# Splitting the weights of a transformer block on GpSimd for each chunk, in place of storing split weights in DRAM

## The chip, the cores and the metric

The kernel runs on one core of a Trainium2 chip. The metric is the time of one execution on the device in microseconds (us), as the median of several runs.

## The reference, cut to what matters

One block on x of shape [1, 2048, 512], all in float32: a layer norm that is scaled and shifted by rows made from a condition c, attention with 32 heads of width 16, a second modulated norm, and a gated feed-forward part of width 1792 (SwiGLU).

```python
mod = (_silu(c) @ w_mod).reshape(c.shape[0], 6, 1, -1)
sa, ca, ga, sb, cb, gb = (mod[:, i] for i in range(6))
h = _layernorm(x) * (1 + ca) + sa
x = x + ga * attention(h, wqkv, wo)          # softmax over all 2048 keys, 32 heads
h = _layernorm(x) * (1 + cb) + sb
x = x + gb * ((silu(h @ w_gate) * (h @ w_up)) @ w_down)
```

## The kernel before, in words

**Split operands.** Dense products run on TensorE (PE) in the type float32r. To keep float32 accuracy each operand is kept as two tiles, a high part `hi` (the value rounded to float32r by a copy) and a low part `lo` (the value minus `hi`), and each product is three matmuls: hi·hi, hi·lo, lo·hi. Making the two parts is "splitting": one copy and one subtraction.

**Tiling.** The 2048 rows are four chunks of 512 (`NC`, `CW`). First comes the projection to q, k and v, which go to DRAM in split form. Attention then runs in 32 units (`NU`): 8 groups of 4 heads for each chunk. A unit has 16 steps; in a step PE makes four score tiles for the row maximum 21 steps ahead (L479, reduced by VectorE, DVE, at L481), four score tiles for the current keys (L506, exponentials on ScalarE, ACT, L508) and the products with v (L521). `kop` and `qop` hold the keys and queries of a unit; half of their loads are issued by GpSimd (POOL) and half by SyncE (SP) at L404.

**Chunk work between the attention steps.** When the eight units of a chunk have ended, its output projection with `wo`, its second norm and its feed-forward part are done during the units of the next chunk. `plain(steps)` emits attention steps alone; `filled(places, work)` emits eight pairs of attention matmuls with matmuls of `work` put between them. The feed-forward part of a chunk is a list of jobs: `gate_up(f)` for f = 0 to 13 (gate and up columns of 128, tile `wgu` with gate and up, hi and lo), and `down(m)` for m = 0 to 6, twice for each m (tile `wd` with two blocks of 128 rows, hi and lo). The order is gate_up 0, 1, 2, down 0, gate_up 3, 4, down 1, and so on to gate_up 13, down 6. A gate_up takes two `filled` calls and each half of a down one. In this stage the matmuls are cut in halves of 64 rows (L719). After the last attention step the last seven jobs of chunk 2 and all of chunk 3 run alone (`whole`, full matmuls at L729).

**Tiles and loads.** `wgu` has two buffers, `wd` one, `mid` (the split product of gate and up) three. `load_gu(f + 1)` is issued on SP when gate_up f begins, `load_wd(m + 1)` on SP when down m has ended. In the last chunk six places are used for `wgu`, four of them in `kop` tiles that are free by then, and loads run four ahead. A unit that closes (`close_unit`) sends its sum through DRAM to get it in the shape of a row: SP issues `dn`, `d_dr` and `rb` (L542), then POOL multiplies `on = o * rb` (L548) and stores it (L549).

**Where the split weights come from.** During the first eight units a generator `split_weights` loads the plain weights into `mid` tiles on the POOL queue (L579), multiplies `wo` by ga and `w_down` by gb / 2 (L605, L621), splits them on POOL (copy L583, subtraction L584), and stores hi and lo to DRAM (`wo_dr`, `gu_dr`, `wd_dr`, L587). `after(i)` advances it at three of 16 steps. Each chunk then loads hi and lo, 1 MB for each `wgu` and `wd`, at L646, L652 and L657.

**Other splits.** The product of gate and up is split at L781 and L782: on POOL during attention, on ACT and DVE in `whole`. The attention output of a chunk is split on POOL at L667 and L668, the turned normed rows at L706 and L707.

**Order.** Every engine runs its instructions in the order in which the program emits them, under manual scheduling, and waits by semaphore. A POOL or ACT instruction that waits holds all that are emitted after it.

Of the kernel before, what the change touches and what calls it, by code (L numbers as in the profile page):

```python
# [9 lines left out]
F32 = mybir.dt.float32  # L10
# [9 lines left out]
P = 128  # L20
S = 2048
D = 512
# [4 lines left out]
NK = D // P  # L27
NC = 4
CW = S // NC
NG = H // 4  # L30
NU = NG * NC
NF = F // P
FG = 2
# [9 lines left out]
UG = 16 * NG  # L43
# [11 lines left out]
def run(it):  # L55
    for _ in it:
        pass


def take(it, k):  # L60
    run(islice(it, k))
# [40 lines left out]
def block_kernel(ctx, tc, x, wqkv, wo, w_gate, w_up, w_down, c, w_mod, out):  # L102
    nc = tc.nc
# [447 lines left out]
    def at(i, f):  # L551
        due.setdefault(i, []).append(f)
# [19 lines left out]
    def as_wo(w):  # L572
        return w.rearrange("p (b k) x c -> p b k (x c)", b=2)

    def split_weights():

        def raw(src, k):
            t = tile_mid().bitcast(F32)
            nc.gpsimd.dma_start(t.rearrange("p e c -> p (e c)").rearrange("p (k c) -> p k c", k=k), src)  # L579
            return t  # L580

        def parts(hi, lo, t):
            nc.gpsimd.tensor_copy(hi, t)  # L583
            nc.gpsimd.tensor_sub(lo, t, hi.bitcast(F32))  # L584

        def store(dst, w):
            nc.gpsimd.dma_start(dst, w.bitcast(F32))  # L587

        def cols(m):
            return slice(m * FG * P, (m + 1) * FG * P)  # L590

        srcs = [(wod[:, 2 * k:2 * k + 2, :], 2) for k in range(NK // 2)]
        for m in range(NF // FG):
            srcs += [(wgd[:, :, cols(m)], NK), (wud[:, :, cols(m)], NK), (wdd[:, m * FG:(m + 1) * FG, :], FG)]
        ahead = [raw(*srcs.pop(0)) for _ in range(2)]
        yield

        def following():
            if srcs:
                ahead.append(raw(*srcs.pop(0)))  # L600
            return ahead.pop(0)

        for k in range(NK // 2):
            t = following()
            nc.gpsimd.tensor_mul(t, t, ga_bc[:, None, :].to_broadcast([P, 2, D]))  # L605
            w = tile_gu()
            parts(as_wo(w)[:, 0], as_wo(w)[:, 1], t)
            store(wo_dr[k], as_wo(w))
            yield
        for m in range(NF // FG):  # L610
            ws = [tile_gu() for _ in range(FG)]
            for e in range(2):
                t = following()
                src = t.rearrange("p e c -> p (e c)").rearrange("p (k f c) -> p f k c", k=NK, f=FG)
                for f in range(FG):
                    parts(ws[f][:, 2 * e], ws[f][:, 2 * e + 1], src[:, f])
                    if e:
                        store(gu_dr[m * FG + f], ws[f])
                yield
            t = following()  # L620
            nc.gpsimd.tensor_mul(t, t, gb_bc[:, None, :].to_broadcast([P, FG, D]))  # L621
            w = tile_wd()
            parts(w[:, 0], w[:, 1], t)
            store(wd_dr[m], w)
            yield

    class Chunk:
        def __init__(self, ci, x2, oT, hT):
            self.ci, self.x2, self.oT, self.hT = ci, x2, oT, hT
            self.w, self.wd, self.mid, self.mv, self.nt = {}, {}, {}, None, []  # L630
            self.places, self.ahead, self.loaded = None, 1, set()
            self.jobs = [(gate_up, (0,)), (gate_up, (1,))]
# [10 lines left out]
        def load_wo(self, places=None):  # L643
            self.wo = places or [as_wo(tile_gu()) for _ in range(NK // 2)]
            for k, w in enumerate(self.wo):
                (nc.gpsimd if self.ci == last else nc.sync).dma_start(w.bitcast(F32), wo_dr[k])  # L646

        def load_gu(self, f):
            if f < NF and f not in self.loaded:
                self.loaded.add(f)  # L650
                self.w[f] = self.places[f % len(self.places)] if self.places else tile_gu()
                nc.sync.dma_start(self.w[f].bitcast(F32), gu_dr[f])  # L652

        def load_wd(self, m):
            if m < NF // FG:
                self.wd[m] = tile_wd()
                nc.sync.dma_start(self.wd[m].bitcast(F32), wd_dr[m])  # L657

        def load_o(self, eng, ks=range(NK)):
            for k in ks:  # L660
# [164 lines left out]
    def scaled(ch):  # L825
        ch.load_gu(0)
        ch.norm_scale(nc.gpsimd)
        ch.nt = [tile_mid().bitcast(F32) for _ in range(2)]
        for t in range(4):
            ch.normalize(t)  # L830

    def hook():
        while posts:
            posts.pop(0)()
# [32 lines left out]
    weights2 = split_weights()  # L867

    def after(i):
        nonlocal pf  # L870
        for f in due.pop(i, []):
            f()
        j = i + LEAD
        if j % 16 == 15 and j < n:
            max_rows(j // 16)
        if i == -2:
            run(late)
            sm.finish()
            es_a0.close()
# [90 lines left out]

    at(n - 24, begin_last)
    at(n - 13, lambda: chunks[last].load_o(nc.gpsimd, range(NK - 1)))
    at(n - 11, lambda: chunks[last].split_o(range(NK - 1)))
    outs = [banks[b] for b in FBANKS]
    for ci in range(last):
        plain(STARTS[ci] - done // 4)
        ch = chunks[ci]
        for t0 in (0, 2):
            work = out_pair(ch, t0, outs, True)
            filled(TWO, work)  # L980
            filled(TWO, work)
        side.append(lambda: scaled(ch))
        plain(NORM)
        plain(WIN, [lambda tp, k=k: ch.turned(tp, k) for k in range(NK)])
        if ci == last - 1:
# [8 lines left out]
    chunks[last - 1].load_gu(NF - 2)  # L994
    filled((0,) * 4, iter(()))


    assert done == 4 * n
# [68 lines left out]
```

## Time and profile before

| | us |
|---|---|
| median of 3 runs | 1879.55 (1879.51 to 1881.34) |
| span of the profiled execution, first to last instruction | 1875.6 |
| PE busy | 1846.7 (98%) |
| DVE busy | 1541.8 (82%) |
| ACT busy | 1252.4 (67%) |
| POOL busy | 415.3 (22%) |

The time outside the span, taken as the median minus the span, is about 4.0 us. How to read the rows that follow: a group of instructions has a line, an engine, an operation, the tiles that it writes and reads, the shape, the count, busy us, mean ns of one, and the idle time of the engine in front of it with what ended it. A timeline row has the start, the time that it covers, and in brackets the idle time in front. A matmul's end is modelled, so starts of matmuls are the better clock: in the last stage they are 0.23 us apart.

### The profile page before, as it was taken

How to read it: one execution, taken by the hardware profiler on the slowest of the kernel's cores; microseconds unless marked ns; L12 is line 12 of the kernel's file. 1: busy time of each engine (PE TensorE's matmuls, PEld its weight loads, DVE VectorE, ACT ScalarE, POOL GpSimd, SP SyncE). 2: the span in 40 equal slices, each digit the busy share in tenths (PEclk: the TensorE clock that was granted, in tenths of full speed). 3: DMA queues.
4: the chain of work that ended last, by engine and by line, in shares of the span. 5: the costliest groups of instructions: out<-in, count | busy, mean ns of one | idle time of the engine just before them, and what ended most of it. 6: DMA issues, size and time to landing. Idle time of an engine off the chain costs nothing.

```text
span 1875.6 us, 41002 instructions
## 1 busy us (share of the span) xinstructions
PE 1846.7 (98%) x16996; PEld 1160.4 (62%) x16996; DVE 1541.8 (82%) x2558; ACT 1252.4 (67%) x2406; POOL 415.3 (22%) x498
## 2 busy tenths in 40 slices
PE   7999999999999999999999999999999999999999
PEld 5766444444455766666555667666554566667887
DVE  5548999999999888888999888889999988831643
ACT  4221888888887766777777776677878877674211
POOL 3000454456323211111133111111123011030200
PEclk9999999999999999999999999999999999999999
DMA  8855677766843534554454454453643446243642
GB/s 286 292 198 142 174 183 178 201 167 190 211 86 78 145 102 124 144 124 90 107 124 116 108 127 131 121 122 78 159 86 56 108 92 156 86 159 119 249 180 110
DMA packets 78854, 267.62 MB, mean 143 GB/s; under 512 B 17364, under 2 KB 22484, under 8 KB 57988
## 3 DMA queue, kind: packets, MB, share of 16 engines
q1 hardware_dynamic: 59820, 180.10, 33.0%
q0 software_dynamic: 18160, 84.10, 19.0%
q8 instruction: 133, 2.18, 0.5%
q10 hardware_dynamic: 688, 0.80, 0.1%
q14 instruction: 53, 0.43, 0.1%
HBM read 201.85 MB, written 62.13 MB: 141 GB/s over the span
## 4 chain that ended last, share of the span: by engine, by line
PE 95%; DVE 2%; ACT 2%; DMA 0%; issue 0%; SPq 0%; ACTq 0%; DVEq 0%
PE bank L521 26%; PE bank L506 22%; PE bank L719 19%; PE bank L479 10%; PE bank L729 7%; PE bank L209 7%; DVE mx L481 1%; PE bank L762 1%; PE bank L491 1%; PE bank L162 0%; PE bank L703 0%; DMA wm_ab<-in_w_mod 0%; DVE stt L745 0%; PE bank L279 0%; PE bank L493 0%; PE bank L492 0%
## 5 line engine op out<-in xcount | busy, mean ns | idle before, releaser
L481 DVE TENSOR_REDUCE mx<-bank 128x1 f32<-128x512 f32 x2048 | 1286.5, 682 | 119.5 <-PE bank L479 72.4
L479 PE MATMUL bank<-kop,qop 48*128 48x512 f32 x2048 | 748.0, 432 | 3.6 <-DVE mx L481 3.4
L506 PE MATMUL bank<-qop,kop 50*128 50x512 f32 x2048 | 742.1, 427 | 4.6 <-ACT pt__20499 L508 0.5
L506 PEld LDWEIGHTS bank<-qop,kop 50*128 50x128 f32 x2048 | 347.0, 184 | 305.6 <-issue 63.3
L479 PEld LDWEIGHTS bank<-kop,qop 48*128 48x128 f32 x2048 | 343.9, 184 | 30.7 <-DVE mx L481 14.4
L719 PE MATMUL bank<-act,wgu 64*128 64x512 f32 x1872 | 297.9, 392 | 0.0
L719 PEld LDWEIGHTS bank<-act,wgu 64*128 64x128 f32 x1872 | 188.4, 187 | 30.9 <-DVE m L779 0.3
L548 POOL TENSOR_TENSOR on<-o,rb 128x512 f32<-128x512 f32 x31 | 39.7, 1282 | 442.9 <-DMA rb<-d_dr 304.0
L719 PE MATMUL bank<-wd,mid 64*128 64x512 f32 x912 | 136.5, 397 | 0.0
L781 POOL CAST mid<-m 128x512 fp32r<-128x512 f32 x40 | 24.3, 609 | 430.1 <-PE bank L479 165.5
L719 PEld LDWEIGHTS bank<-wd,mid 64*128 64x128 f32 x912 | 93.3, 185 | 12.0 <-issue 0.8
L209 PE MATMUL bank<-hT,wqs 128*128 128x512 f32 x384 | 95.7, 399 | 2.1 <-DVE prt L369 0.8
L209 PEld LDWEIGHTS bank<-hT,wqs 128*128 128x128 f32 x384 | 70.3, 188 | 24.3 <-issue 6.1
L777 DVE SCALAR_TENSOR_TENSOR q<-th,bank 128x512 f32<-128x512 f32 x56 | 37.7, 673 | 57.4 <-ACT th L773 57.2
L773 ACT ACTIVATE th<-bank 128x512 f32<-128x512 f32 x56 | 33.2, 593 | 58.3 <-PE bank L729 57.9
L793 DVE TENSOR_TENSOR x<-bank,x 128x512 f32<-128x512 f32 x84 | 53.8, 684 | 20.4 <-PE bank L506 20.2
L369 DVE TENSOR_TENSOR prt<-bank,prt 128x512 fp32r<-128x512 f32 x32 | 22.0, 688 | 46.5 <-ACT prt L367 46.5
L367 ACT CAST prt<-bank 128x512 fp32r<-128x512 f32 x32 | 18.8, 587 | 60.2 <-PE bank L209 46.9
L779 DVE TENSOR_TENSOR m<-bank,q 128x512 f32<-128x512 f32 x56 | 38.7, 691 | 21.2 <-PE bank L729 19.1
L729 PE MATMUL bank<-wd,mid 128*128 128x512 f32 x216 | 52.1, 394 | 0.4 <-DVE mid L782 0.3
L782 POOL TENSOR_TENSOR mid<-m,mid 128x512 fp32r<-128x512 f32 x40 | 51.6, 1291 | 3.3
L719 PE MATMUL bank<-wgu,act 64*128 64x512 f32 x288 | 47.7, 394 | 0.1
(6282 smaller groups left out, 5155.0 us busy)
## 6 DMA issues: line engine op xcount, KB each, us to landing
wgu<-gu_dr SPq DMA_DIRECT2D x48, 1024.0 KB
wd<-wd_dr SPq DMA_DIRECT2D x28, 1024.0 KB
kop<-kd SPq DMA_DIRECT2D x33, 768.0 KB
kop<-kd POOLq DMA_DIRECT2D x29, 768.0 KB, 8.5
gu_dr<-wgu POOLq DMA_DIRECT2D x14, 1024.0 KB, 14.1
kd<-prt SPq DMA_DIRECT2D x16, 512.0 KB
qd<-prt SPq DMA_DIRECT2D x16, 512.0 KB
kop<-gu_dr SPq DMA_DIRECT2D x8, 1024.0 KB
```

What stands on the lines that cost most here:

```text
L209: nc.tensor.matmul(pt, lhs(a, k), rhs(b, k), start=(n == 0), stop=(n == 3 * nk - 1))
L479: nc.tensor.matmul(pm, qop[u][rows, s, qt * P:(qt + 1) * P], kop[u % 3][rows, s, kc * CW:(kc + 1) * CW], start=True, stop=True)
L481: nc.vector.tensor_reduce(mx[u][:, b, s, qt, kc:kc + 1], pm, op=ALU.max, axis=AX.X)
L506: nc.tensor.matmul(sp, kop[u % 3][rows, h // 2, kt * P:(kt + 1) * P], qop[u][rows, h // 2, :], start=True, stop=True)
L521: nc.tensor.matmul(pv[u][32 * h:32 * h + 32, cols], v_flat[:, e0:e0 + 32], p_[h][:, cols], start=(kt == 0 and half == 0), stop=(kt == 15), ...
L548: mul.tensor_mul(on, o, rb)
L719: nc.tensor.matmul(outs[e], lhs(e, a, k)[rows], rhs(b, k)[rows], start=(ph == 0 and j == 0), stop=(j == z and (ph == 1 or trade is not None)),
L729: nc.tensor.matmul(outs[e], lhs(e, a, k), rhs(b, k), start=(j == 0), stop=(j == z))
L777: nc.vector.scalar_tensor_tensor(q, th, 1.0, outs[0], op0=ALU.add, op1=ALU.mult)
L779: nc.vector.tensor_mul(m32, outs[1], q)
L782: (nc.gpsimd if slow else nc.vector).tensor_sub(mid[:, 1, :], m32, mid[:, 0, :].bitcast(F32))
L793: nc.vector.tensor_add(ch.x2[:, t, :], outs[e], ch.x2[:, t, :])
```

## The change

Plain weights take the place of split ones in DRAM, and each chunk splits them itself.

1. `relay_weights` takes the place of `split_weights`. It copies the plain gate and up columns from DRAM to DRAM into the layout of a tile (28 transfers on the POOL queue), and loads, scales and stores `wo` and `w_down` (9 products on POOL). It is advanced at two of 16 steps instead of three. There are no splits in it.
2. `load_gu`, `load_wd` and `load_wo` load the plain weights, half the bytes, into the place of the low part.
3. `halves` splits in place: `hi` is copied from the loaded part, then the loaded part is made `lo` by subtracting `hi`. It runs on POOL, or, where `alone` is set, copies on ACT and subtracts on DVE.
4. The split of `wgu` f + 1 is emitted in the middle of gate_up f, that of `wd` behind gate_up f for odd f, that of `wo` one step ahead of the split of the attention output, all on POOL. Chunk 0 to 2 have their first `wgu` split after the norm.
5. In `whole`, chunk 2's last `wgu` (f = 13) and `wd` (m = 6), and chunk 3's `wgu` 0 and 1 and all seven `wd` are split on ACT and DVE; chunk 3's `wgu` 2 to 13 on POOL, three ahead.

Of 92 splits (four chunks of 14, 7 and 2), 81 are on POOL and 11 on ACT and DVE. The order of the matmuls on PE is the same in both kernels.

```diff
-    gu_dr = dram.tile([NF, P, 4, NK, P], F32, name="gu_dr")
-    wd_dr = dram.tile([NF // FG, P, 2, FG, D], F32, name="wd_dr")
-    wo_dr = dram.tile([NK // 2, P, 2, 2, D], F32, name="wo_dr")
+    gu_dr = dram.tile([NF, P, 2, NK, P], F32, name="gu_dr")
+    wd_dr = dram.tile([NF // FG, P, FG, D], F32, name="wd_dr")
+    wo_dr = dram.tile([NK // 2, P, 2, D], F32, name="wo_dr")
...
+    def relay_weights():
+        def raw(src):
+            t = tile_mid().bitcast(F32)
+            nc.gpsimd.dma_start(t, src)
+            return t
+        def scaled_out(dst, t, row):
+            nc.gpsimd.tensor_mul(t, t, row[:, None, :].to_broadcast([P, 2, D]))
+            nc.gpsimd.dma_start(dst, t)
+        srcs = [(wo_dr[k], wod[:, 2 * k:2 * k + 2, :], ga_bc) for k in range(NK // 2)]
+        srcs += [(wd_dr[m], wdd[:, m * FG:(m + 1) * FG, :], gb_bc) for m in range(NF // FG)]
+        ahead = []
+        for j in range(len(srcs) + 1):
+            if j < len(srcs):
+                ahead.append(raw(srcs[j][1]))
+            if j:
+                dst, _, row = srcs[j - 1]
+                scaled_out(dst, ahead.pop(0), row)
+            for f in range(2 * j - 2, 2 * j):
+                if 0 <= f < NF:
+                    for e, w in enumerate((wgd, wud)):
+                        nc.gpsimd.dma_start(gu_dr[f, :, e], w[:, :, f * P:(f + 1) * P])
             yield
...
-                nc.sync.dma_start(self.w[f].bitcast(F32), gu_dr[f])
+                nc.sync.dma_start(self.w[f][:, 1::2].bitcast(F32), gu_dr[f])
+        def halves(self, hi, lo, alone):
+            (nc.scalar.copy if alone else nc.gpsimd.tensor_copy)(hi, lo.bitcast(F32))
+            (nc.vector if alone else nc.gpsimd).tensor_sub(lo, lo.bitcast(F32), hi.bitcast(F32))
+        def split_gu(self, f, alone=False):
+            if f < NF and f not in self.split:
+                self.split.add(f)
+                self.halves(self.w[f][:, 0::2], self.w[f][:, 1::2], alone)
...
+            at(i + 8, lambda: chunks[u // NG].split_wo())
             at(i + 9, lambda: chunks[u // NG].split_o())
...
-        if 0 <= i < UG and i % 16 in (3, 5, 8):
+        if 0 <= i < UG and i % 8 == 3:
             next(weights2, None)
...
             work = job(ch, *args, outs, True)
-            for places in (TWO, TWO) if job is gate_up else (DOWN,):
-                filled(places, work)
+            if job is not gate_up:
+                filled(DOWN, work)
+                continue
+            filled(TWO, work)
+            ch.split_gu(args[0] + 1)
+            filled(TWO, work)
+            if args[0] % FG:
+                ch.split_wd(args[0] // FG)
...
             for _ in job(ch, *args, banks[b:b + 2], False):
                 yield
             hook()
+            if job is gate_up:
+                f = args[0]
+                ch.split_gu(f + (3 if ch.ci == last else 1), ch.ci != last)
+                if f % FG:
+                    ch.split_wd(f // FG, True)
...
             ch.turned(banks[6 + e], k + e, nc.vector if k else nc.gpsimd)
         take(rest, 6)
+        for f in range(k, k + 2):
+            ch.split_gu(f, k == 0)
```

More of the change, by code (lines that the diff above doesn't have):

```diff
@@ L573, in as_wo @@
         return w.rearrange("p (b k) x c -> p b k (x c)", b=2)
-    def split_weights():
-        def raw(src, k):
+    def relay_weights():
+        def raw(src):
             t = tile_mid().bitcast(F32)
-            nc.gpsimd.dma_start(t.rearrange("p e c -> p (e c)").rearrange("p (k c) -> p k c", k=k), src)
+            nc.gpsimd.dma_start(t, src)
             return t
[L582 to L624, printed above, removed]
@@ L631, in __init__ @@
             self.places, self.ahead, self.loaded = None, 1, set()
+            self.split, self.parted = set(), set()
             self.jobs = [(gate_up, (0,)), (gate_up, (1,))]
@@ L645, in load_wo @@
             for k, w in enumerate(self.wo):
-                (nc.gpsimd if self.ci == last else nc.sync).dma_start(w.bitcast(F32), wo_dr[k])
+                (nc.gpsimd if self.ci == last else nc.sync).dma_start(w[:, 1].bitcast(F32), wo_dr[k])
         def load_gu(self, f):
@@ L651, in load_gu, with split_wd, split_wo @@
                 self.w[f] = self.places[f % len(self.places)] if self.places else tile_gu()
-                nc.sync.dma_start(self.w[f].bitcast(F32), gu_dr[f])
+                nc.sync.dma_start(self.w[f][:, 1::2].bitcast(F32), gu_dr[f])
[6 more added lines that the diff above has]
+                self.halves(self.w[f][:, 0::2], self.w[f][:, 1::2], alone)
+        def split_wd(self, m, alone=False):
+            if m not in self.parted:
+                self.parted.add(m)
+                self.halves(self.wd[m][:, 0], self.wd[m][:, 1], alone)
+        def split_wo(self):
+            for w in self.wo:
+                self.halves(w[:, 0], w[:, 1], False)
         def load_wd(self, m):
@@ L656, in load_wd @@
                 self.wd[m] = tile_wd()
-                nc.sync.dma_start(self.wd[m].bitcast(F32), wd_dr[m])
+                nc.sync.dma_start(self.wd[m][:, 1].bitcast(F32), wd_dr[m])
         def load_o(self, eng, ks=range(NK)):
@@ L830, in scaled @@
             ch.normalize(t)
+        ch.split_gu(0)
     def hook():
@@ L865, in block_kernel @@
     at(UG - 2, lambda: chunks[0].load_wo())
-    weights2 = split_weights()
+    weights2 = relay_weights()
     def after(i):
@@ L972, in block_kernel @@
     at(n - 13, lambda: chunks[last].load_o(nc.gpsimd, range(NK - 1)))
+    at(n - 14, lambda: chunks[last].split_wo())
     at(n - 11, lambda: chunks[last].split_o(range(NK - 1)))
@@ L991, in block_kernel @@
             work = job(ch, *args, outs, True)
-            for places in (TWO, TWO) if job is gate_up else (DOWN,):
-                filled(places, work)
-    chunks[last - 1].load_gu(NF - 2)
+            if job is not gate_up:
[6 more added lines that the diff above has]
+                ch.split_wd(args[0] // FG)
+    ch.load_gu(NF - 2)
+    ch.split_wd(NF // FG - 2)
     filled((0,) * 4, iter(()))
+    ch.split_gu(NF - 2)
     assert done == 4 * n
```

## The prediction, made before the change was run

> **What bounds the kernel now.** I read the page first, for the engines' shares and the chain of work that ended last.
>
> ```profile
> span 1875.6 us, 41002 instructions
> ...
> PE 1846.7 (98%) x16996; PEld 1160.4 (62%) x16996; DVE 1541.8 (82%) x2558; ACT 1252.4 (67%) x2406; POOL 415.3 (22%) x498
> ...
> PE 95%; DVE 2%; ACT 2%; DMA 0%; issue 0%; SPq 0%; ACTq 0%; DVEq 0%
> ```
>
> PE carries 95% of the chain and POOL none of it. An average over stages hides which limit holds where, so next comes busy time by stretch, and the row maxima (L481) alone in two of the stretches.
>
> ```profile
> core 0: us, PE busy (x) PEld busy (x) DVE busy (x) ACT busy (x) POOL busy (x), PEclk, DMA share, GB/s
> 310.00:360.00 50.00, 50.00 (x504) 23.45 (x504) 49.63 (x85) 43.99 (x88) 29.15 (x32) 1.00 0.77 184
> 700.00:750.00 50.00, 50.00 (x522) 34.87 (x520) 44.09 (x70) 34.86 (x69) 5.68 (x6) 1.00 0.48 123
> 910.00:960.00 50.00, 49.86 (x508) 23.13 (x504) 49.89 (x85) 44.19 (x88) 14.00 (x18) 1.00 0.66 155
> ```
>
> ```profile
> 310.00:360.00 50.00, 49.41 (x83) 1.00 0.77 184
> 910.00:960.00 50.00, 49.76 (x83) 1.00 0.66 155
> ```
>
> Attention steps alone (the first and third stretch) are bound by DVE: 49.6 and 49.9 of 50 us. Where chunk work lies between the steps (700 to 750 us), PE is full and DVE has 6 of 50 us left. The clock column is 1.00 throughout. The third view is what PE itself waits for, from 560 to 1700 us, the longest first (us in total, times, longest):
>
> ```profile
> PE bank L479 <- DVE mx L481: 1.9, 6, 0.3
> ```
>
> The waits listed below it name ACT; no matmul there waits for a DMA or POOL. So less traffic and less work on POOL early on have no wait on PE to remove, while a new wait in front of a matmul adds in full.
>
> **The change part by part.** Prices first, from the views of single tiles and lines (ns of one: min/median/max).
>
> ```profile
> L583 POOL CAST wd<-mid x7: 1037/1038/1041, 262.3 to 498.6; 128x1024 fp32r<-128x1024 f32 x7
> L584 POOL TENSOR_TENSOR wd<-mid,wd x7: 2373/2378/2391, 263.4 to 499.7; 128x1024 fp32r<-128x1024 f32 x7
> ```
>
> ```profile
> L782 POOL TENSOR_TENSOR mid<-m,mid x40: 1275/1291/1304, 623.8 to 1746.2; 128x512 fp32r<-128x512 f32 x40
> L782 DVE TENSOR_TENSOR mid<-m,mid x16: 692/693/1377, 1734.8 to 1866.8; 128x512 fp32r<-128x512 f32 x16
> ```
>
> ```profile
> L781 POOL CAST mid<-m x40: 604/607/613, 623.2 to 1745.5; 128x512 fp32r<-128x512 f32 x40
> ```
>
> ```profile
> L781 ACT CAST mid<-m x16: 612/621/621, 1734.1 to 1866.1; 128x512 fp32r<-128x512 f32 x16
> ```
>
> A split of 1024 columns on POOL costs 1.04 + 2.38 and some 0.1 us between, 3.5 us; 81 of them are 284 us. On ACT and DVE no row has 1024 columns: a copy lies between 0.62 and 1.24 us, a subtraction between 0.69 and 1.39. POOL's copy grows by 1038/607 = 1.71 and its subtraction by 2378/1291 = 1.84 from 512 to 1024 columns; with these I take 1.06 us on ACT and 1.28 us on DVE.
>
> *First eight units.* POOL loses all splits there and gains 28 transfers; loads fall to half. POOL is 29.2 of 50 us busy from 310 us and 14.0 from 910, yet both stretches hold 83 maxima. So I cost this at nothing: the maxima on DVE hide it. If the relay made keys late, DVE would idle as long; keys are loaded most of a unit ahead.
>
> *Splits during attention.* They hold nothing on DVE that bounds (same two rows). The question is POOL's queue: a split that stands behind L548, which waits for `rb`, can be late for its gate_up. The tightest place is gate_up 1 of a chunk whose gate_up 0 starts as a unit closes:
>
> ```profile
> 609.64 0.42 SPq L652 DMA_DIRECT2D wgu<-gu_dr  x1
> 610.23 0.32 SPq L657 DMA_DIRECT2D wd<-wd_dr  x1
> 610.74 0.56 SPq L542 DMA_DIRECT2D rb<-d_dr  x1
> ```
>
> ```profile
> 619.87 1.29 POOL L548 TENSOR_TENSOR on<-o,rb 128x512 f32<-128x512 f32 x1 [8.43 <-DMA rb<-d_dr]
> 621.46 0.61 POOL L549 DMA_DIRECT2D o_dr<-on  x1 [0.30 <-POOL on L548]
> ```
>
> ```profile
> 623.17 0.69 PE L719 MATMUL bank<-act,wgu 64*128 64x512 f32 x4
> ```
>
> ```profile
> 1436.94 0.56 SPq L542 DMA_DIRECT2D rb<-d_dr  x1
> ```
>
> ```profile
> 1441.77 1.28 POOL L548 TENSOR_TENSOR on<-o,rb 128x512 f32<-128x512 f32 x1 [4.12 <-DMA rb<-d_dr]
> ```
>
> POOL is free at 622.07, so the split ends at 625.6, 2.4 us after PE wants it at 623.17 (the low part is wanted some 0.5 us later, so about 2 us are lost). But `rb` took 9.1 us behind two loads of 1 MB, and 4.8 us with none ahead at 1436.94; with half the bytes ahead I take the middle, 7.0 us, and the 2 us are back. I take 0.7 us over the three chunks; from zero to 3 x 2.5 = 7.5 us.
>
> The two splits of `wo`, 7.0 us, stand ahead of the split of the attention output, here for chunk 0:
>
> ```profile
> 540.21 1.29 POOL L668 TENSOR_TENSOR act<-act,act 128x512 fp32r<-128x512 f32 x1
> ```
>
> ```profile
> 547.94 0.49 PE L719 MATMUL bank<-wgu,act 64*128 64x512 f32 x2
> ```
>
> The last of its four then ends at 541.50 + 7.0 = 548.5. PE starts on the first at 547.94 and reaches the last some 3 us later, so it is hidden with about 2.5 us to spare; a later `wo` load would cost one for one. The key loads behind on POOL (L404) and the load of chunk 3's x, now behind two splits, move back by as much; their data are wanted a good part of a unit later, so I cost them at nothing, one for one if that cover fails.
>
> *End of attention to the last chunk.* Here the splits on ACT and DVE are in program order behind other work.
>
> ```profile
> 1742.02 5.66 PE L729 MATMUL bank<-act,wgu 128*128 128x512 f32 x24
> ```
>
> ```profile
> 1748.31 1.62 PE L729 MATMUL bank<-wd,mid 128*128 128x512 f32 x6
> ```
>
> ```profile
> 1755.34 0.85 PE L729 MATMUL bank<-kop,wgu 128*128 128x512 f32 x3
> ```
>
> ```profile
> 1743.89 1.53 ACT L695 ACTIVATE v_flat<-v_flat,rs,rs 128x512 f32<-128x512 f32 x2 [8.64 <-DVE rs L691]
> ```
>
> ```profile
> 1749.49 0.61 ACT L781 CAST mid<-m 128x512 fp32r<-128x512 f32 x1
> ```
>
> ```profile
> 1746.21 1.29 POOL L782 TENSOR_TENSOR mid<-m,mid 128x512 fp32r<-128x512 f32 x1
> ```
>
> ```profile
> 1750.14 1.38 DVE L782 TENSOR_TENSOR mid<-m,mid 128x512 fp32r<-128x512 f32 x1 [1.12 <-ACT mid L781]
> ```
>
> (a) Chunk 2's gate_up 13 starts at 1742.02. Its split is emitted behind L695, the normed rows, which wait for DVE until 1743.89. The copy thus runs 1745.42 to 1746.48. The subtraction meets POOL's L782, which ends at 1747.50; two such meet at 1750.14, where DVE's took 1.38 in place of 0.69 us. I let it wait: 1747.50 + 1.28 = 1748.78. The third matmul, the first with the low part, would have begun at 1742.49: 6.3 us lost (5.3 without the meeting; 4.2 to 7.0 with the copy's and subtraction's ends). The ACT and DVE work queued behind is for gate_up 13 and later.
>
> (b) Down 6 of chunk 2 began at 1748.31, 0.6 us after gate_up 13. Now it needs `wd` 6, whose copy is queued behind the `mid` copy that ends at 1750.10: 1751.16 in the old time. Its subtraction follows DVE's L782, which ends at 1751.52, and one POOL copy of 0.5 us left: to 1753.3. From the second matmul there are 5 more steps of 0.23, eight transposes of 0.11 and 18 matmuls before gate_up 0 of chunk 3: 1.15 + 0.9 + 4.15 = 6.2, so 1759.2 in place of 1755.34: 3.9 us (2.5 to 5). Splits of `wgu` 0 and 1 fit into this.
>
> ```profile
> 1865.21 6.27 PE L729 MATMUL bank<-wd,mid 128*128 128x512 f32 x24
> ```
>
> ```profile
> 1866.13 0.62 ACT L781 CAST mid<-m 128x512 fp32r<-128x512 f32 x1 [2.81 <-DVE m L779]
> ```
>
> ```profile
> 1866.79 0.69 DVE L782 TENSOR_TENSOR mid<-m,mid 128x512 fp32r<-128x512 f32 x1 [0.69 <-ACT mid L781]
> ```
>
> (c) The last down 6 has the same chain at the very end: `wd` copy 1866.75 to 1867.81, subtraction to 1869.09, then 22 steps of 0.23 and the last matmul's 0.39: 1874.5 against 1871.48, 3.1 us (2.0 to 3.4).
>
> (d) In chunk 3 POOL splits `wgu` while DVE subtracts:
>
> ```profile
> 1784.39 0.69 DVE L782 TENSOR_TENSOR mid<-m,mid 128x512 fp32r<-128x512 f32 x1 [0.69 <-ACT mid L781]
> ```
>
> ```profile
> 1788.30 1.07 PE L729 MATMUL bank<-wd,mid 128*128 128x512 f32 x4
> ```
>
> Alone, the `wd` split there would end at 1784.37 + 1.06 + 1.28 = 1786.7, with 1.8 us left before its low part is wanted at 1788.5. One POOL subtraction (2.38) in the way takes that and up to 1.5 us more, at four downs. I take 1.5 us, from 0 to 6.
>
> [...]
>
> **Sum**: 6.3 + 3.9 + 3.1 + 1.5 + 0.7 = 15.5 us on 1875.6, and the 4.0 us outside the span make 1895.0 (median before: 1879.55). A gain or loss below 0.2%, 3.8 us, could not be told from none.
>
> **Rivals.**
> - *Queue.* The loads do not bring `rb` forward, and POOL's splits are late for PE during attention: 7.5 in place of 0.7, 1902. For: L548 was the last wait in the rows at 619.87. Against: `rb` took half the time with nothing ahead.
> - *Port.* Each DVE subtraction of the last chunk meets a POOL one: (d) is 6, 1899.5. For: the 1.38 us; against: the row at 1784.39 has its lone 0.69, and two splits to a down fill 7 us of POOL.
> - *Cheap end.* ACT and DVE are quicker than the rows scale to and the meetings fail: 4.2 + 2.5 + 2.0, 1888 or a little less.
> - *Faster.* In the DVE-bound stage POOL's splits slow the maxima after all. The place is the 147 steps of attention ahead of chunk 0's work, 588 maxima. It wins once each is 15.5 us / 588 = 26 ns quicker; at 36 ns it gives 1895.0 - 21 = 1874. For it: 15 us more of POOL in 50. Against: the equal 83.
> - *It does not do what it says*: split weights are still stored. The order of POOL's instructions has no split before the first chunk and 81 behind, so I give this no chance of its own.
>
> **How the numbers follow.** Forecast 0.60, queue 0.15, port 0.11, cheap end 0.07, faster 0.04, an unseen cover that leaves it within 0.2% 0.03. Slower is 0.60 + 0.15 + 0.11 + 0.07 = 0.93. The range from 1887 to 1904 takes in queue and port and most of the cheap end.
>
> **What would show it.** Right: gate_up 13 of chunk 2 has its third matmul some 6 us after the first could have begun, with PE waiting for the DVE subtraction of `wgu`; the last down 6 waits for the `wd` subtraction; maxima keep their 83 in 50 us; PE waits for POOL in attention are below 2 us. Wrong: waits on POOL of several us at L712, or idle DVE in the first units, or no wait at L722.

## The result, and the profile after the change

The changed kernel takes 1903.46 us (median of 4 runs, 1900.47 to 1905.37), the kernel before 1879.80 us beside it (4 runs, 1879.51 to 1881.34): a ratio of 1.0124, 95% interval 1.0109 to 1.0138, slower by 23.7 us. The profiled execution took 1904.07 us on a span of 1902.3, so 1.8 us lie outside the span.

The page of the changed kernel, first its span and its busy times:

```profile
span 1902.3 us, 41185 instructions
...
PE 1858.8 (98%) x16996; PEld 1167.5 (61%) x16996; DVE 1570.2 (83%) x2569; ACT 1263.3 (66%) x2417; POOL 615.3 (32%) x586
```

POOL has 200 us more work and PE, with the same 16996 matmuls, 12.1 us more busy time. The second number needs a reason, since nothing was added on PE. The stretches that the prediction used, of the changed kernel (busy us of each engine, granted clock, DMA share and GB/s), and the row maxima alone in two of them:

```profile
310.00:360.00 50.00, 50.00 (x502) 23.45 (x494) 49.62 (x85) 43.94 (x87) 17.61 (x20) 1.00 0.72 176
700.00:750.00 50.00, 50.00 (x528) 34.63 (x522) 43.83 (x71) 34.42 (x68) 15.93 (x12) 1.00 0.39 84
910.00:960.00 50.00, 49.85 (x506) 23.32 (x494) 49.64 (x85) 43.27 (x86) 20.42 (x22) 1.00 0.57 126
```

```profile
310.00:360.00 50.00, 49.41 (x83) 1.00 0.72 176
910.00:960.00 50.00, 49.54 (x83) 1.00 0.57 126
```

The attention stage stands as it was: 83 maxima in 50 us, DVE full where it was full. The stretches of the last stage (busy PE, PEld, DVE, ACT, POOL, then the clock) are different:

```profile
1740.00:1760.00 20.00, 13.70 (x48) 10.10 (x47) 14.08 (x34) 3.05 (x4) 3.34 (x4) 0.83 0.17 53
1760.00:1780.00 20.00, 15.92 (x66) 12.87 (x65) 12.22 (x12) 6.94 (x9) 14.56 (x12) 0.83 0.45 157
...
1880.00:1900.00 20.00, 14.61 (x55) 10.98 (x53) 7.45 (x10) 2.16 (x3) 0.00 (x0) 0.91 0.22 78
```

Two things are seen in the 40 us from 1740: PE is idle for 10.4 us, and the clock column is 0.83 and not 1.00. The timeline of PE over that stage names both (start, time covered, count, and in brackets the idle time ahead with what ended it). First the kernel before, from 1734, then the changed one:

```profile
1736.51 5.67 PE L729 MATMUL bank<-wd,mid 128*128 128x512 f32 x24
...
1747.52 1.03 PE L703 MATMUL bank<-ident,v_flat 128*128 128x128 f32 x8
...
1859.72 5.66 PE L729 MATMUL bank<-kop,wgu 128*128 128x512 f32 x24
```

```profile
1739.67 5.76 PE L722 MATMUL bank<-wd,mid 128*128 128x512 f32 x24
1750.83 1.22 PE L722 MATMUL bank<-act,wgu 128*128 128x512 f32 x2 [5.39 <-ACT wgu L630]
1752.96 7.43 PE L722 MATMUL bank<-act,wgu 128*128 128x512 f32 x22 [0.91 <-DVE wgu L631]
1760.23 1.03 PE L696 MATMUL bank<-ident,v_flat 128*128 128x128 f32 x8
1763.87 0.47 PE L722 MATMUL bank<-wd,mid 128*128 128x512 f32 x1 [2.60 <-POOL kop L700]
1765.82 2.50 PE L722 MATMUL bank<-wd,mid 128*128 128x512 f32 x5 [1.48 <-DVE wd L631]
...
1774.59 5.62 PE L722 MATMUL bank<-kop,wgu 128*128 128x512 f32 x24
...
1881.35 5.63 PE L722 MATMUL bank<-kop,wgu 128*128 128x512 f32 x24
1889.36 0.51 PE L722 MATMUL bank<-wd,mid 128*128 128x512 f32 x1 [2.38 <-ACT wd L630]
1890.62 7.13 PE L722 MATMUL bank<-wd,mid 128*128 128x512 f32 x23 [0.75 <-DVE wd L631]
```

The waits are those that the prediction named: gate_up 13 of chunk 2 behind its split, and the down 6 of either chunk behind its own. (The 2.60 is put down to POOL's `kop` at L700, which down 6 does not read; ACT's copy of `wd`, which it does read, ends 0.1 us before the matmul, at 1763.77, as this row of ACT's timeline shows.)

```profile
1762.72 1.05 ACT L630 CAST wd<-wd 128x1024 fp32r<-128x1024 f32 x1
```

What was not named: 22 matmuls of gate_up 13 cover 7.43 us, where 24 covered 5.66 before. Behind each long wait the matmuls come 0.43 us apart in place of 0.23, which is also why PE has more busy time for the same matmuls. So the same stage is cut once more, at the edges of the clock record, each stretch at half clock with the 3.41 us ahead of it (busy PE, clock):

```profile
1747.18:1750.59 3.41, 0.00 (x0) 1.00 0.74 278
1750.60:1757.42 6.82, 5.68 (x13) 0.50 0.00 0
...
1760.83:1764.25 3.42, 0.82 (x6) 1.00 0.65 229
1764.25:1771.07 6.82, 5.34 (x17) 0.50 0.53 193
...
1887.13:1890.54 3.41, 0.51 (x1) 1.00 0.00 0
1890.54:1893.95 3.41, 3.33 (x8) 0.50 0.00 0
```

Half clock lasts 6.8, 6.8 and 3.4 us, and each time it follows a stretch in which PE waited and was busy for 0.82 us or less of 3.41.

The difference can be laid out by the starts of the same matmuls in the two timelines: up to down 5 of chunk 2, 1739.67 - 1736.51 = 3.2 us; from there to the transposes 12.7 - 3.2 = 9.5 (gate_up 13); to gate_up 0 of chunk 3 (1774.59 against 1755.34) 6.5 (down 6); to the last gate_up 13 (1881.35 against 1859.72) 2.4 (chunk 3); to the end of the last down 6, 1897.75 against 1871.48, 4.6. Together 26.3 of the 26.7 us between the two spans. The profiled execution of before, 1875.6 + 1.8 = 1877.4 us, lies 2.4 us under its median of 1879.80, the one of after 0.6 over, hence 23.7 between the medians.

### The profile page after: what moved, and what is told of

It reads as the page before. It is cut to its first block, busy times and chain, and to the rows that moved or that the text cites. A ratio compares the mean times of both kernels' runs of the same rounds, so it can differ in the third digit from the quotient of the medians.

```text
span 1902.3 us, 41185 instructions
## 1 busy us (share of the span) xinstructions
PE 1858.8 (98%) x16996; PEld 1167.5 (61%) x16996; DVE 1570.2 (83%) x2569; ACT 1263.3 (66%) x2417; POOL 615.3 (32%) x586
## 3 DMA queue, kind: packets, MB, share of 16 engines
q1 hardware_dynamic: 66988, 132.91, 26.7%
## 4 chain that ended last, share of the span: by engine, by line
PE 93%; DVE 3%; ACT 2%; DMA 1%; issue 1%; SPq 0%; ACTq 0%; DVEq 0%
PE bank L521 26%; PE bank L506 22%; PE bank L712 19%; PE bank L479 9%; PE bank L722 7%; PE bank L209 6%; DVE mx L481 1%; PE bank L491 1%; PE bank L696 0%; DVE stt L738 0%; PE bank L755 0%; PE bank L162 0%; PE bank L279 0%; DMA wm_ab<-in_w_mod 0%; DVE wd L631 0%
## 5 line engine op out<-in xcount | busy, mean ns | idle before, releaser
L631 POOL TENSOR_TENSOR wgu<-wgu 128x1024 fp32r<-128x1024 f32 x51 | 123.5, 2422 | 4.2
L630 POOL CAST wgu<-wgu 128x1024 fp32r<-128x1024 f32 x51 | 54.2, 1062 | 97.0 <-DMA wgu<-gu_dr 72.9
L722 PE MATMUL bank<-wd,mid 128*128 128x512 f32 x216 | 56.7, 416 | 8.0 <-DVE wd L631 3.0
L404 POOL DMA_DIRECT2D kop<-kd x29 | 17.0, 585 | 146.4 <-PE bank L506 103.4
```

The source lines that it names most:

```text
L630: (nc.scalar.copy if alone else nc.gpsimd.tensor_copy)(hi, lo.bitcast(F32))
L631: (nc.vector if alone else nc.gpsimd).tensor_sub(lo, lo.bitcast(F32), hi.bitcast(F32))
L722: nc.tensor.matmul(outs[e], lhs(e, a, k), rhs(b, k), start=(j == 0), stop=(j == z))
```

## The experiments

The theory after the comparison: PE waits for the last splits in program order, and each long wait is paid a second time by a stretch at half clock. Rivals: W, the half clock has nothing to do with the waits; U, the loss is made in the attention stage or by POOL elsewhere; Port, POOL's splits slow DVE's subtractions in chunk 3.

| kernel | median, us | ratio to before, 95% interval |
|---|---|---|
| changed | 1903.46 | 1.0124 (1.0109 to 1.0138) |
| busy_pe | 1896.29 | 1.0094 (1.0080 to 1.0107) |
| early_gu13 | 1893.99 | 1.0078 (1.0065 to 1.0091) |
| early_wd6 | 1891.96 | 1.0069 (1.0057 to 1.0082) |
| early_both | 1885.63 | 1.0033 (1.0021 to 1.0046) |
| own_places | 1883.93 | 1.0023 (1.0013 to 1.0033) |
| no_pool_last | 1881.45 | 1.0011 (1.0000 to 1.0021) |
| relay_shift | 1881.24 | 1.0009 (1.0000 to 1.0018) |
| pool_more | 1884.72 | 1.0033 (1.0020 to 1.0046) |
| stalls_before | 1904.45 | 1.0131 (1.0118 to 1.0144) |
| stalls_equal | 1910.00 | 1.0156 (1.0140 to 1.0172) |

The kernel before beside them had medians of 1878.99 (busy_pe and the three early ones), 1879.18 (relay_shift, pool_more) and 1879.93 (own_places, no_pool_last and the two with put-in waits); beside the changed kernel it was 1879.80.

### busy_pe: the same waits with PE at work

```diff
+            idle = {(gate_up, (NF - 1,), last - 1): 20, (down, (NF // FG - 1, 0), last - 1): 10,
+                    (down, (NF // FG - 1, 0), last): 10}.get((job, args, ch.ci), 0)
+            for _ in range(idle):
+                nc.tensor.matmul(banks[b], ch.hT[0][:, 0, 0:P], ch.hT[0][:, 0, :], start=True, stop=True)
             for _ in job(ch, *args, banks[b:b + 2], False):
```

> The changed kernel with 40 more matmuls on PE whose result is overwritten: 20 ahead of chunk 2's gate_up 13, 10 ahead of each down 6, so that PE is busy in the time in which it waits (5.4, 2.6 and 2.4 us). Nothing else is moved; every wait on ACT and DVE stays. Theory: the waits stay and the half-clock windows behind them go, some 2 us at each of three places: 1903.5 - 6 = 1897.5, clock 1.0 in the record at 1750, 1764 and 1890. Rival W: the windows do not hang on the waits: 1903.5, or up to 1 us more where the added matmuls run past the end of a wait.

Measured 1896.29. The stretches of the last stage (PE, PEld, DVE, ACT, POOL, clock):

```profile
1740.00:1760.00 20.00, 17.80 (x79) 13.56 (x77) 14.01 (x31) 6.99 (x10) 6.29 (x8) 1.00 0.31 102
1760.00:1780.00 20.00, 18.95 (x87) 15.69 (x88) 12.84 (x15) 4.91 (x8) 17.92 (x15) 1.00 0.53 187
```

and its PE timeline at gate_up 13 and at the end of the last down 6:

```profile
1743.43 4.72 PE L1011 MATMUL bank<-act 128*128 128x512 f32 x20
...
1750.20 5.40 PE L722 MATMUL bank<-act,wgu 128*128 128x512 f32 x22 [1.42 <-DVE wgu L631]
...
1884.13 5.63 PE L722 MATMUL bank<-wd,mid 128*128 128x512 f32 x23 [0.77 <-DVE wd L631]
```

Forty useless matmuls make the kernel 6 us faster by the ratios and 7 by the medians. The clock is 1.00, the waits for DVE are still there, and the 22 matmuls take 5.40 us in place of 7.43, the last 23 take 5.63 in place of 7.13. W falls: the half clock at these three places comes from PE's idle time, and it costs about as much as the theory said (1897.5).

### early_gu13, early_wd6, early_both: the splits emitted earlier

`early_gu13` adds the first of these edits, `early_wd6` the second, `early_both` both:

```diff
         if t % 2:
             add_o(ch, t - 1, banks[t - 1:t + 1], False)
+        if t == 1:
+            chp.split_gu(NF - 1, True)
...
-            for _ in job(ch, *args, banks[b:b + 2], False):
+            for j, _ in enumerate(job(ch, *args, banks[b:b + 2], False)):
                 yield
+                if job is gate_up and args[0] == NF - 1 and j == 11:
+                    ch.split_wd(NF // FG - 1, True)
```

> Only the split of chunk 2's gate_up 13 is emitted earlier, between the two halves of the output projection's sums, ahead of the normed rows. Theory (PE's waits in the last stage, and half-clock windows that follow each long wait): gate_up 13 loses its waits of 5.56 + 1.32 us and its 22 slow steps (2.1 us), 9.0 in all: 1903.5 - 9.0 = 1894.5, and the granted clock is 1.0 at gate_up 13. Rival W (the windows at half clock come on their own and not from the waits): only 6.9 us go, 1896.6, and a window at half clock remains near 1750. Rival U (the loss is made by POOL's splits in the attention stage): no change, 1903.5.

Measured 1893.99: gate_up 13 has no wait and is at full clock (its 24 matmuls cover 5.76 us). The theory's 1894.5 fits better than W's 1896.6, which lies 0.5 us outside the interval (1.0065 to 1.0091 of 1878.99 is 1891.2 to 1896.1), too little to decide alone. Down 6 still waits, 3.23 us ahead of its first matmul, with half clock behind that wait.

> Only the split of wd 6 is emitted earlier, in the middle of gate_up 13 (both chunks that run alone), ahead of ACT's tanh and of the mid copy. Theory: down 6 of chunk 2 loses its waits of 2.84 + 1.64 us and about 2.0 us at half clock, the last down 6 its 2.5 + 1.0 us and about 2.0 at half clock: 12 us in all, 1891.5; the windows near 1764 and 1890 are gone. Rival W: 8 us go, 1895.5, windows remain. Rival U: no change, 1903.5. If the weights of wd 6 land too late for the middle of gate_up 13, ACT's tanh waits for them and less than 12 us goes.

Measured 1891.96, as the theory said; 1895.5 lies outside the interval (1.0057 to 1.0082 of 1878.99 is 1889.7 to 1894.4).

> Both splits are emitted earlier. Theory: 9 + 12 = 21 us go, 1882.5, that is 2.7 us above the kernel before (the rest lies in the attention stage, 3.2 us by the aligned matmuls); no half clock between 1740 and 1880. Rival W: 15 us, 1888.5. Rival U: 1903.5. A rival that POOL's port slows DVE's subtractions in the last chunk by more than 1.5 us would leave it at 1885 or above.

Measured 1885.63, 3 us above the theory and 3 below W. The PE timeline shows what is left at down 6 of chunk 2:

```profile
1751.55 2.08 PE L722 MATMUL bank<-wd,mid 128*128 128x512 f32 x5 [1.82 <-DVE wd L631]
1753.43 1.91 PE L696 MATMUL bank<-ident,v_flat 128*128 128x128 f32 x8
```

I had taken it that the low part would be ready with gate_up 13's end. With gate_up 13 earlier, the subtraction now stands behind DVE's four sums of down 5 and ends after PE gets there; the wait of 1.82 us is again followed by slow steps (eight transposes in 1.91 us, 1.03 at full clock), where no half clock was expected. The time also meets the sign that was set for Port (1885 or above), which this run leaves open. U falls: two moved splits bring back some 17 of 24 us.

### stalls_before, stalls_equal: waits put into the kernel before

```diff
             for _ in job(ch, *args, banks[b:b + 2], False):
                 yield
+            if job is gate_up and ch.ci == last:
+                f = args[0] + 1
+                for _ in range({4: 5, 6: 7, 8: 9, 10: 11, 12: 13}.get(f, 0)):
+                    nc.scalar.copy(ch.w[f][:, 0], ch.w[f][:, 0].bitcast(F32))
             hook()
```

In `stalls_equal` the count is 8 for each even f below 14.

> The kernel before, with 5, 7, 9, 11 and 13 copies of a weight tile onto itself on ACT ahead of the last chunk's gate_up 4, 6, 8, 10 and 12, so that PE waits there for ACT some 0.62 us per copy less the 2.2 us that the gate_up ahead covers: about 0.9, 2.1, 3.4, 4.6 and 5.9 us, 17 in all. Theory (a wait that leaves a 3.4 us window of the clock record less than about half busy is followed by a window at half clock, and by a second one where PE starts again in the middle of the first): no half clock behind the 0.9, one or two windows behind each of the last three, at 1.7 us to 3.4 us of loss each: 1879 + 17 + 7 = 1903. Rival W (waits cost themselves and the clock goes its own way): 1896. Rival N (the half clock needs a whole idle window): windows only behind 4.6 and 5.9, 1900.

> The kernel before, with 8 copies on ACT ahead of the last chunk's gate_up 2, 4, 6, 8, 10 and 12: six equal waits of about 2.8 us, 17 in all, which fall at different places of the 3.4 us windows. Theory: half clock follows those that lie in one window (busy share under about half) and not those that are shared by two windows; some 3 of 6, 2 us each: 1879 + 17 + 6 = 1902. Rival W: 1896, with no tie between the place and the clock. Rival N: no half clock, as no window is wholly idle, 1896.

Measured 1904.45 and 1910.00. The gate_ups behind the waits in the PE timeline of stalls_before; one without a wait covers 5.66 us:

```profile
1783.59 5.79 PE L729 MATMUL bank<-kop,kop 128*128 128x512 f32 x24 [1.11 <-ACT kop L1009]
...
1802.77 7.26 PE L729 MATMUL bank<-kop,wgu 128*128 128x512 f32 x24 [2.41 <-ACT wgu L1009]
...
1824.72 8.16 PE L729 MATMUL bank<-kop,kop 128*128 128x512 f32 x24 [3.71 <-ACT kop L1009]
...
1848.88 8.03 PE L729 MATMUL bank<-kop,kop 128*128 128x512 f32 x24 [5.01 <-ACT kop L1009]
...
1874.21 7.37 PE L729 MATMUL bank<-kop,wgu 128*128 128x512 f32 x24 [6.30 <-ACT wgu L1009]
```

A wait of 1.11 us costs little beyond itself (0.13). One of 2.41 costs 1.6 us more, and longer ones between 1.7 and 2.5 more, not in proportion to their length. In stalls_equal five of six waits of 3.06 us are followed by a slow gate_up (7.12 to 8.51 us), more than the 3 that I expected, and one is not:

```profile
1789.60 8.51 PE L729 MATMUL bank<-kop,kop 128*128 128x512 f32 x24 [3.06 <-ACT kop L1009]
...
1854.73 5.77 PE L729 MATMUL bank<-kop,kop 128*128 128x512 f32 x24 [3.06 <-ACT kop L1009]
```

Its clock record tells them apart. In the changed kernel half clock starts at 1750.60, 1764.25 and 1890.54 us; the second lies 13.65 us after the first and the third 139.94, 4 and 41 times the same 3.41 us (13.65 / 4 and 139.94 / 41). So a run's record is laid out here in cells of 3.41 us, counted from a change of its own clock. The cells in which these two waits lie and the stretch behind the first (busy PE, clock):

```profile
1785.29:1788.70 3.41, 1.25 (x6) 1.00 1.02 430
1788.70:1795.52 6.82, 5.92 (x14) 0.50 0.19 80
...
1850.13:1853.55 3.42, 1.54 (x7) 1.00 0.76 316
1853.55:1856.96 3.41, 2.23 (x10) 1.00 0.00 0
```

The first wait leaves a cell with 1.25 us of PE, and half clock follows; the other is shared by two cells with 1.54 and 2.23 us and is followed by none. N falls, since no cell was wholly idle; W falls with the times (1879.93 plus 18.5 us of waits is 1898.4; the interval starts at 1902.1). The measured 1910.00 is 8 us above what I expected of stalls_equal, and its profiled execution, 1904.92, is the fastest of four. That the waits fall at other places of the cells in the slower three would explain the rest, but they left no trace, so this is not shown.

A gap of 2.41 us was enough (stalls_before: the clock is 0.50 from 1803 to 1806 us, behind it), and so was a cell in which PE was busy for 1.25 of 3.41 us (stalls_equal).

### own_places, no_pool_last: what is left when PE no longer waits

`own_places` puts chunk 2's last two splits on POOL and gives wd 6 its own places:

```diff
+        def own_wd(self, m, hi, lo):
+            self.wd[m] = hi, lo
+            nc.sync.dma_start(lo.bitcast(F32), wd_dr[m])
...
+                if ch.ci == last and f == 8:
+                    w = kop[(NU - 3) % 3][:, 0, :].rearrange("p (b f d) -> p b f d", b=2, f=FG)
+                    ch.own_wd(NF // FG - 1, w[:, 0], w[:, 1])
+                if ch.ci == last and f == 11:
+                    ch.split_wd(NF // FG - 1)
...
     ch.load_x2(nc.gpsimd)
+    chp.own_wd(NF // FG - 1, *(pb.tile([P, FG, D], F32R, name="qop", tag="qop", bufs=3) for _ in range(2)))
+    chp.split_wd(NF // FG - 1)
...
     take(rest, 48)
+    chp.split_gu(NF - 1)
     for t in range(4):
         out_terms(ch, t, banks[t], (NK - 1,))
```

`no_pool_last` also has all of chunk 3's splits of `wgu` on ACT and DVE:

```diff
-                ch.split_gu(f + (3 if ch.ci == last else 1), ch.ci != last)
+                ch.split_gu(f + (3 if ch.ci == last else 1), True)
...
-            ch.split_gu(f, k == 0)
+            ch.split_gu(f, True)
```

> The changed kernel, with chunk 2's last two splits on POOL, which is idle for 23 us there, and wd 6 of chunks 2 and 3 loaded early into places of their own (two query tiles and a key tile that are free by then). Theory: no wait of PE for a split of gate_up 13 or down 6 is left; of the 24 us by which the changed kernel is slower remain some 2 us of the attention stage and 1 us in the last chunk: 1879 + 3 = 1882, no half clock before the end. Rival U (something else of the change costs in the last stage, such as POOL's subtractions in the way of DVE's): as with both splits early, 1885.6 or more.

> As own_places, and all splits of the last chunk's wgu on ACT and DVE in place of POOL. Theory: DVE's subtractions lose their meetings with POOL's, worth at most 1 us; DVE gets 1.22 us more in each gate_up of 5.7 us and has room for it: 1880.5 to 1883 against 1882. Rival Port (the meetings cost several us in the last chunk): 3 us or more faster than own_places. Rival (DVE or ACT becomes late): slower than own_places by 2 us or more, with waits of PE on DVE at L722.

Measured 1883.93 and 1881.45. The waits of PE from 1730 us on fall from 14.3 us in the changed kernel (5.4, 3.0, 2.6, 2.4 and 0.9) to 1.0 us in own_places, all on DVE's subtraction of `wd`. That subtraction, in the rows of tile `wd` (ns min/median/max), first of own_places, then of no_pool_last:

```profile
L631 DVE TENSOR_TENSOR wd<-wd x6: 1226/2054/2057, 1772.6 to 1857.1; 128x1024 fp32r<-128x1024 f32 x6
```

```profile
L631 DVE TENSOR_TENSOR wd<-wd x6: 1218/1220/1227, 1772.8 to 1854.5; 128x1024 fp32r<-128x1024 f32 x6
```

own_places lies 2 us above the theory's 1882, and its interval (1882.4 to 1886.1) holds U's 1885.6 as well; what speaks for the theory are the waits and a clock of 1.00 up to the last matmul. Alone the subtraction takes 1.22 us, beside POOL's splits 2.05. The worst meeting is one of the `mid` subtraction, 0.69 us alone, in own_places (DVE's timeline, then POOL's):

```profile
1787.62 2.89 DVE L779 TENSOR_TENSOR mid<-m,mid 128x512 fp32r<-128x512 f32 x1 [0.69 <-ACT mid L778]
```

```profile
1787.55 2.41 POOL L631 TENSOR_TENSOR wgu<-wgu 128x1024 fp32r<-128x1024 f32 x1
```

POOL starts 0.07 us ahead and DVE ends 0.55 us after POOL: DVE's took 2.20 us more than its 0.69 alone, most of POOL's 2.41. Without POOL in chunk 3 DVE has more work and the last gate_up 13 still starts earlier, first in own_places, then in no_pool_last:

```profile
1865.66 5.63 PE L726 MATMUL bank<-kop,wgu 128*128 128x512 f32 x24
```

```profile
1863.05 5.63 PE L726 MATMUL bank<-kop,wgu 128*128 128x512 f32 x24
```

2.61 us less here and 0.28 at down 5 of chunk 2 (1738.62 against 1738.34) make 2.3 us for the meetings of the two engines: more than the 1 us that I expected, and less than the 3 us of Port. The times agree (2.5 us) within intervals that overlap. From the start of down 5 to the end of the last matmul no_pool_last takes 136.4 us, the kernel before 135.0. By the medians 1.5 us (0 to 3.9 by the interval) are left over the kernel before. No version beats it.

### relay_shift, pool_more: the attention stage

```diff
-        if 0 <= i < UG and i % 8 == 3:
+        if 0 <= i < UG and i % 16 in (4, 14):
...
-            (nc.scalar.copy if alone else nc.gpsimd.tensor_copy)(hi, lo.bitcast(F32))
+            for _ in range(1 if alone or self.ci == last else 2):
+                (nc.scalar.copy if alone else nc.gpsimd.tensor_copy)(hi, lo.bitcast(F32))
```

The first edit is relay_shift, the second pool_more, each on no_pool_last.

> As no_pool_last, and the relay of the plain weights is advanced at steps 4 and 14 of 16 in place of 3 and 11, so that its transfers from DRAM to DRAM no longer start in the step after the row maxima are loaded (at step 10). Theory: the wait of 0.8 us on the load of the maxima seen once near 267 us goes, some 0.5 us, too little for the times: 1881, by the aligned matmuls 0.3 to 1.0 us less by 280 us. Rival: the 2 us that are left over the kernel before come from the relay: 1879.5 or less. Rival: they come from the attention stage's splits on POOL: no change.

> As no_pool_last, and each split of chunks 0 to 2 on POOL does its copy twice (the second writes the same values), 1.04 us more for each of some 70 splits, 73 us of POOL in all. Theory (a split is hidden as long as it ends before its gate_up; the rows show some with 0 to 3 us to spare, most with more): a few us, 1881.5 + 3 = 1884.5, and the waits show PE behind POOL's wgu at L726. Rival Queue (POOL's queue is at its limit, each us more is paid): 1881.5 + 40 or more. Rival (any work on POOL is free in this stage): 1881.5.

Measured 1881.24: no gain that could be told, though the interval (1879.2 to 1882.6) does not rule out the rival's 1879.5. The wait on the load of the maxima, a 0.8 us wait of PE in the changed kernel, is not there, but no_pool_last did not have it either, so this run settles nothing about it. Instead it has a stretch at half clock with PE full, beside the same stretch of no_pool_last (below it; PE busy, clock):

```profile
986.00:1000.00 14.00, 13.75 (x108) 0.76 0.10 35
```

```profile
986.00:1000.00 14.00, 13.43 (x126) 1.00 0.11 38
```

pool_more measured 1884.72, 3.3 us more. Its POOL is busy for 61 us more from 560 to 1700 us (490.3 in place of 429.3). A new row appears among PE's waits (us in total, times, longest):

```profile
PE bank L717 <- POOL wgu L632: 1.5, 3, 0.6
```

So the theory's 1884.5 holds: one us more for each split is mostly hidden, 3.3 of 61 are paid, and a POOL queue that is already at its limit is out. A few splits come within 1 us of being late. But these waits are not most of the price. In the profiled execution down 5 of chunk 2 starts 6.4 us later than in no_pool_last (1744.69 against 1738.34), and 4.8 of them arise behind 1700 us, at the output projection, where no_pool_last has no wait:

```profile
1738.31 0.73 PE L760 MATMUL bank<-kop,kop 128*128 128x512 f32 x2 [0.97 <-ACT kop L665]
1740.70 4.15 PE L760 MATMUL bank<-kop,kop 128*128 128x512 f32 x10 [1.66 <-DVE kop L666]
```

DVE's subtraction of `kop` (L666) took 2.36 us there beside a split on POOL of 2.35, and ten matmuls at half clock follow the wait. So part of the price is again a meeting of the two engines and a wait that is paid twice.

## Why the prediction was right, and where it was too small

It gave 1895.0 us, with a range from 1887 to 1904; the time is 1903.46, at the upper end. That the range holds it is partly luck: its upper end was drawn for Queue and Port, and half clock was no term of it. The direction and the places were right, and the idle times of PE nearly to the tenth. By the starts of the same matmuls, which is what the prediction computed, each split was later than that:

- **(a)** gate_up 13: 6.3 us predicted for its third matmul. The idle time is 5.39 + 0.91 = 6.3, but the matmul came 7.3 us late (1752.96, less 3.2, against 1742.49), since the normed rows ahead of the copy on ACT began 1.3 us later than in the kernel before (1748.32, less 3.2, against 1743.89). With the half clock behind it the stage lost 9.5. (The upper end of 7.0 does not follow from the prediction's own ends: 1747.50 + 1.39 gives 6.4.)
- **(b)** down 6 of chunk 2: 3.9 predicted, though its own terms give 4.2 (1753.3 + 6.2 is 1759.5 and not 1759.2). Idle 2.60 + 1.48 = 4.1, the second matmul 4.6 late, lost 6.5. The meetings with POOL that (a) and (b) put in, 1.0 and 0.5 us, were there and cost a little less: DVE's subtraction of `wgu` took 2.05 us (at 1750.86, beside L775 on POOL from 1750.56 to 1751.83), that of `wd` 1.63 (at 1764.14, beside L699 on POOL to 1764.68), 0.83 and 0.41 more than the 1.22 alone.
- **(c)** the last down 6: 3.1 predicted, idle 2.38 + 0.75 = 3.1, the second matmul 3.5 late, lost 4.6.
- **(d)** chunk 3: 1.5 predicted, 2.4 measured. The mechanism is the one named, DVE's subtraction held by POOL's (2.05 in place of 1.22 us): from gate_up 0 to the last gate_up 13 the kernel before takes 104.4 us, the changed one 106.8, own_places 107.3, and no_pool_last, without POOL's splits, 104.8. Its prices were close: 1.06 us on ACT was 1.05, 1.28 on DVE was 1.22.
- **(e)** the attention stage: 0.7 predicted, 3.2 us by the start of down 5 in the profiled pair. One pair overstates it. Down 5 starts at 1736.01 and 1735.15 us in the two kernels with put-in waits, which are the kernel before up to there, and between 1736.89 and 1738.86 in six other runs with the attention stage of the changed kernel. By the means the stage costs 2.5 us, and each of the seven starts later than each of the three. The 0.8 us wait on the maxima near 267 us is in the changed kernel's profile alone at that length (0 to 0.4 us in the six). The loss grows along the whole stage, and its cause stays open.

The step that failed is the pricing of a wait by its length alone, in (a), (b) and (c): the sum counted how late the next matmul starts and then went on at 0.23 us a matmul. The clock column had been read as 1.00 throughout, which held for a kernel whose PE hardly waited, and the prediction carried it over to one that waits. What this left out can be read beside busy_pe. From the first matmul with the low part to the next common point (the transposes, gate_up 0 of chunk 3, the end) the changed kernel takes 7.27, 8.77 and 7.13 us, busy_pe at full clock 5.23, 6.34 and 5.63: 6.0 us. This is shown by busy_pe (waits filled, clock 1.00, 6 to 7 us gone) and by the two kernels with put-in waits. The other terms that were too small are the splits themselves, 15.4 us late in place of 13.3, (d) by 0.9 and (e) by 1.8.

A smaller slip is the 4.0 us outside the span: they were the median of other executions less this span. 1.8 us lie outside, and the profiled execution was 2.2 us faster than the median of 1879.55; the two add to the same 4.0, so the forecast did not suffer.

The rivals: Queue gave 1902, near the time, by a mechanism that is wrong; PE waited for POOL's `wgu` in the attention stage hardly at all, and some 17 of the 24 us came back with two splits moved in the last stage. Port was right in its mechanism and gave 4.5 us more than (d), where 0.9 were measured. The row at 1784.39, which the prediction held against it, says nothing of it: POOL was busy for 0.00 us from 1775 to 1850 us in the kernel before. Cheap end and Faster did not occur: the maxima kept their 83 in 50 us.

## What to carry to other kernels

A wait put in front of PE was not priced by its length in these runs: on a PE that was otherwise full, waits from 2.4 us up cost 1.5 to 2.9 us more (with one exception in ten, 0.1), through the half clock behind them. So add that to each long wait, or keep PE busy with something during it. Work that was moved from an early, idle place to just ahead of its use was nearly free where another engine set the pace (some 2.5 us for the whole attention stage), and was paid in full in the last stage (15.4 us late at three places), where program order puts it behind the work that PE is waiting for. An engine that is idle (POOL, 23 us at the end of the attention) can be a better place for it than the one with the shorter instruction; own_places shows this together with earlier loads of `wd`, so not for the engine alone.

## What the runs showed that I had not expected

- The half clock did not need an idle cell of 3.41 us. It followed each cell with 1.25 us of PE or less in the rows above. Near half busy it went either way: in early_both a cell with 1.59 us was followed by it, in stalls_equal one with 1.54 was not. In the rows above it lasted one cell where PE started 0.08 us into the cell (1890.62 in the changed kernel), and two where it started 0.90 us in (1789.60 in stalls_equal) or had its last wait end 1.57 and 2.36 us in (1765.82 and 1752.96 in the changed kernel).
- Stretches of half clock also appear with PE full, away from any long wait, in 8 of the 12 profiles: near 990 us in the changed kernel, early_both and relay_shift, near 1404 in early_gu13, early_wd6 and stalls_equal, near 191 in pool_more and stalls_before. In relay_shift 108 matmuls fill 14 us in place of 126. By the starts of the same matmuls that one, of 6.8 us, cost 2.0 us, the two others near 990, of 3.4 us, 0.5 each. What sets them off stays open. The three behind the waits of the changed kernel are not of this kind, since busy_pe does away with them.
- A run-to-run spread of several us is not a mark of waits on PE alone: stalls_equal ran from 1904.92 to 1913.30 us, but own_places, with 1.0 us of waits in the last stage, from 1880.17 to 1888.18, and the kernel before beside both from 1876.62 to 1886.98.
